# Attention and gated FFN in one kernel: joint q/k loads, causal masks on two engines, x flips in FFN banks, and a new plan of the order

## The chip, the cores and the metric

The kernel runs on one core of one Trainium2 chip. The time is the device time of one execution in microseconds (us), as the median of several executions. One execution does 64 heads of causal attention with decay, and then a gated FFN over 4,608 tokens.

The engines are called by the profile's names: PE is TensorE (matmul), PEld its weight load, DVE VectorE, ACT ScalarE, POOL GpSimd, SP SyncE.

## The reference, cut to what matters

```python
B, H, S, D = 8, 8, 576, 64                          # q, k, v: [B, H, S, D]; f: [B, H, S]
scores = (q @ k.T) / sqrt(D)
cum    = cumsum(log(clip(f, 1e-4, 1)), -1)
scores = where(causal, -1e9, scores + cum[..., :, None] - cum[..., None, :])
attn   = softmax(scores)                            # the maximum is taken off first
x      = (attn @ v) -> [B*S, H*D] = [4608, 512]
g      = x @ w_gate                                 # [4608, 1536]
out    = (g * sigmoid(g) * (x @ w_val)) @ w_out     # [4608, 512]
```

## The kernel before: the parts that the change touches

The program is not written in its order of execution. Each piece of work is an `op` with a modelled duration, the ops it must follow, the buffers it takes and a priority (`key`). A small event simulation (`Plan`) then decides on the host in which order each engine's instructions are emitted. So a changed duration in the model, or a changed constant, moves instructions on every engine. Cuts are marked.

```python
# two heads ("a pair") of q or k per load, from GpSimd's queue
def ld_qk(e, p, nm, b):
    nc.gpsimd.dma_start(out=nat[b.pool][b.i],
        in_=srcs[nm][2 * p : 2 * p + 2].rearrange("h (p t) d -> p h (t d)", t=QT))

# "turn": q or k is transposed on TensorE; "straighten": PSUM -> QK on ScalarE or VectorE
bn, bt = Buf("natw" if b == 1 else "nat"), Buf("t", ("f", BORROW), ("s", 22.0))
o1 = op(("POOL", 0.64), ld_qk, p, nm, bn, take=[bn], key=kk, dma=0.74, ...)
o3 = op(("PE", mm(*[QP] * QT)), turn, bn, bt, after=[o1, o_id], take=[bt], use=[bn], ...)
# ... cut

# one bank of scores: matmul -> exp -> causal mask -> weighing of V
a = op(("PE", mm(*cols)), score, h, i, bs, ...)
a = op(("ACT", act(sum(cols))), expo, h, i, bs, ...)
a = op(("POOL", 0.33), mask, h, i, after=[a], use=[hp], key=kk, ...)     # affine_select on GpSimd
ws.append(op(("PE", mm(*[D + 1] * cells)), weigh, h, i, bo, base, opens, ...))
# ... cut: reciprocal and scaling on VectorE

# "flip": the scaled result is transposed on TensorE and put into xT, which the FFN reads
bt = Buf("t", ("f", BORROW))           # one bank "t"; an FFN bank "f" only until BORROW
a = op(("PE", mm(*[P] * nq)), flip, bx, bt, qb, nq, after=scaled + [o_id], take=[bt], use=[bx], ...)

# idle-filling matmuls on the identity, emitted while the plan sees TensorE without work
def dummy(i):
    z = bank[bank_of["f"] + i]
    nc.tensor.matmul(z[:, :HALF], ident, ident.unsqueeze(1).to_broadcast([P, 2, P]), start=True, stop=True)
span = plan.run((2.0, IDLE_TO, dummy, 0.107))
```

Later on each FFN column chunk needs one chunk of `wg` and `wv` (384 KB each, four chunks, loaded from GpSimd's queue). A "gate" is the group of matmuls with `wg` and `wv`, a "projection" that with `wo`.

The softmax here doesn't subtract the row's maximum and nothing guards it: scores larger than these inputs give would overflow.

## Time and profile before

| kernel before | value |
|---|---|
| median of 3 runs | 405.83 us (403.91 to 407.4) |
| span of the profiled execution | 1431.7 us, not one of the timed runs' kind |
| masks on GpSimd | 256: 192 of one block, 64 of two |
| q/k loads of batches 0 to 2 | 24, two heads each |

Read this page with care: TensorE ran at a quarter of its pace in the profiled execution, which the prediction finds from the matmul durations. The rows below are from the groups of the page and from its loads. The columns are line, engine, operation, output and inputs with shapes, count, then busy us and the mean ns of one; in the load rows the last figure is the median us from issue to landing.

```profile
L662 PE MATMUL ps<-xT,wv 128*128 128x512 bf16 (+3 forms) x480 | 388.7, 1020 | 0.0
...
L547 POOL TENSOR_SCALAR_AFFINE_SELECT PT<-PT 128x128 bf16<-128x128 bf16 (+1 forms) x192 | 52.5, 274 | 473.2 <-ACT PT L538 469.5
L547 POOL TENSOR_SCALAR_AFFINE_SELECT PTa<-PTa 128x256 bf16<-128x256 bf16 x64 | 25.9, 405 | 461.5 <-ACT PTa L538 461.4
...
wg<-in_moe_w_gate_dram POOLq DMA_DIRECT2D x4, 384.0 KB, 7.6
wv<-in_moe_w_val_dram POOLq DMA_DIRECT2D x4, 384.0 KB, 9.3
```

What may be used of such a page: durations of engines other than TensorE (a mask is 0.274 or 0.405 us), and counts. What may not: waits. At this pace TensorE is busy 99% of the span, and the others mostly wait for it.

### The profile page before, as it was taken

The numbers are of one execution on the slowest core, as the hardware profiler recorded it, in microseconds if no ns is written. First come the engines' busy times: TensorE is split into PE (matmuls) and PEld (weight loads), VectorE is DVE, ScalarE is ACT, GpSimd is POOL, SyncE is SP. The second block draws the span as 40 slices with busy tenths as digits, with TensorE's granted clock in tenths as the row PEclk, the third lists the DMA queues.
The fourth block names the chain that finished last, engine by engine and source line by source line (L and its number), as shares of the span: only waits on it lengthen the run. The fifth ranks groups of instructions, "written<-read, shape, count | busy, mean of one in ns | idle before, by whom it ended". The sixth has DMA issues, their size and how long they took to land.

```text
span 1431.7 us, 8507 instructions
## 1 busy us (share of the span) xinstructions
PE 1424.2 (99%) x3189; PEld 569.1 (40%) x3189; DVE 233.2 (16%) x447; ACT 237.5 (17%) x444; POOL 135.1 (9%) x370
## 2 busy tenths in 40 slices
PE   9999999999999999999999999999999999999998
PEld 6665553344433333343343343434443222222332
DVE  3132220122101210112002110121101210210210
ACT  3322210122112111111111212212221000100000
POOL 5311120101000100010001101100110000000000
DMA  8510210330034003400233012200000000000000
GB/s 140 93 35 9 44 25 22 59 67 0 8 79 76 0 0 79 98 1 17 50 72 64 16 21 51 56 0 1 8 15 8 0 8 22 0 0 29 0 0 26
DMA packets 103897, 46.57 MB, mean 33 GB/s; under 512 B 87792, under 2 KB 98736, under 8 KB 103536
## 3 DMA queue, kind: packets, MB, share of 16 engines
q1 hardware_dynamic: 89440, 31.08, 9.5%
q0 software_dynamic: 11296, 14.16, 6.4%
q10 hardware_dynamic: 3120, 0.79, 0.3%
q8 instruction: 25, 0.41, 0.1%
q14 instruction: 16, 0.13, 0.0%
HBM read 38.34 MB, written 15.78 MB: 38 GB/s over the span
## 4 chain that ended last, share of the span: by engine, by line
PE 99%; POOL 0%; issue 0%; ACT 0%; ACTq 0%; POOLq 0%
PE ps L662 49%; PE ps L677 25%; PE ps L530 11%; PE ps L561 7%; PE ps L585 2%; PE ps L763 2%; PE ps L418 2%; POOL xT L412 0%; ACT ot L681 0%; POOL ident masks.py:199 0%; POOL ident masks.py:197 0%; ACTq L681 0%; POOLq L802 0%
## 5 line engine op out<-in xcount | busy, mean ns | idle before, releaser
L662 PE MATMUL ps<-xT,wv 128*128 128x512 bf16 (+3 forms) x480 | 388.7, 1020 | 0.0
L662 PE MATMUL ps<-xT,wg 128*128 128x512 bf16 (+3 forms) x480 | 387.7, 1016 | 0.0
L677 PE MATMUL ps<-wo,hh 128*128 128x512 bf16 (+1 forms) x444 | 382.9, 1098 | 0.0
L530 PE MATMUL ps<-QK 68*128 68x320 bf16 (+4 forms) x448 | 210.2, 637 | 0.0
L662 PEld LDWEIGHTS <-wv 128*128 128x128 bf16 x480 | 104.5, 221 | 194.5 <-issue 193.1
L662 PEld LDWEIGHTS <-wg 128*128 128x128 bf16 x480 | 99.8, 212 | 199.1 <-issue 198.3
L677 PEld LDWEIGHTS <-hh 128*128 128x128 bf16 (+1 forms) x444 | 94.1, 216 | 206.4 <-issue 204.9
L666 ACT ACTIVATE th<-ps 128x512 f32<-128x512 f32 (+3 forms) x120 | 66.5, 554 | 527.8 <-PE ps L662 527.8
L561 PEld LDWEIGHTS <-PT 128*128 128x128 bf16 x768 | 106.7, 186 | 77.4 <-issue 65.8
L538 ACT ACTIVATE PT<-ps 128x512 bf16<-128x512 f32 (+2 forms) x192 | 96.7, 508 | 242.5 <-PE ps L530 237.1
L670 DVE SCALAR_TENSOR_TENSOR th<-th,ps 128x512 f32<-128x512 f32 (+3 forms) x120 | 75.6, 630 | 357.6 <-ACT th L666 357.5
L673 DVE TENSOR_TENSOR hh<-th,ps 128x512 bf16<-128x512 f32 (+3 forms) x120 | 76.1, 634 | 273.5 <-PE ps L662 273.4
L561 PE MATMUL ps<-VB,PT 128*128 128x65 bf16 x768 | 120.0, 350 | 0.0
L530 PEld LDWEIGHTS <-QK 68*128 68x128 bf16 x448 | 78.5, 197 | 69.6 <-issue 67.4
L547 POOL TENSOR_SCALAR_AFFINE_SELECT PT<-PT 128x128 bf16<-128x128 bf16 (+1 forms) x192 | 52.5, 274 | 473.2 <-ACT PT L538 469.5
L547 POOL TENSOR_SCALAR_AFFINE_SELECT PTa<-PTa 128x256 bf16<-128x256 bf16 x64 | 25.9, 405 | 461.5 <-ACT PTa L538 461.4
L568 DVE RECIPROCAL rc<-ps 128x5 f32<-128x5 f32 (+2 forms) x64 | 12.4, 194 | 328.5 <-PE ps L561 328.4
L681 ACT ACTIVATE ot<-ps 128x512 f32<-128x512 f32 (+1 forms) x37 | 22.1, 597 | 256.0 <-PE ps L677 256.0
L538 ACT ACTIVATE PTa<-ps 128x384 bf16<-128x384 f32 x64 | 31.1, 490 | 130.3 <-PE ps L530 128.5
L561 PEld LDWEIGHTS <-PTa 128*128 128x128 bf16 x192 | 32.1, 194 | 47.0 <-issue 37.0
L585 PEld LDWEIGHTS <-xn 128*128 128x128 bf16 x160 | 33.9, 235 | 33.8 <-issue 32.1
L585 PE MATMUL ps<-ident,xn 128*128 128x128 bf16 x160 | 43.2, 493 | 0.0
(48 smaller groups left out, 295.3 us busy)
## 6 DMA issues: line engine op xcount, KB each, us to landing
out_dram<-ot SPq DMA_DIRECT2D x35, 256.0 KB
natv<-in_v_dram SPq DMA_DIRECT2D x29, 256.0 KB
qk_d<-in_q_dram POOLq DMA_DIRECT2D x5, 576.0 KB, 5.5
qk_d<-in_k_dram POOLq DMA_DIRECT2D x5, 576.0 KB, 5.8
wg<-in_moe_w_gate_dram POOLq DMA_DIRECT2D x4, 384.0 KB, 7.6
wv<-in_moe_w_val_dram POOLq DMA_DIRECT2D x4, 384.0 KB, 9.3
wo<-in_moe_w_out_dram POOLq DMA_DIRECT2D x4, 384.0 KB, 6.3
QK<-qk_d SPq DMA_TRANSPOSE x80
```

The source lines that it names most:

```text
L418: nc.tensor.transpose(t[:, n : n + QP], src[:, h, P * y : P * y + P], ident[:QP, :QP])
L530: nc.tensor.matmul(s[:, c : c + w], QK[:KR, hqk[p].i, 2 * j + 1, kt * P : (kt + 1) * P], QK[:KR, hqk[p].i, 2 * j, q0 : q0 + w], start=True ...
L538: nc.scalar.activation(place(h, i)[:, OFFS[i] : OFFS[i] + c], ps(bs)[:, :c], AF.Exp, scale=0.125)
L547: nc.gpsimd.affine_select(out=d, in_=d, pattern=pat, compare_op=ALU.is_ge, fill=0.0, base=0, channel_multiplier=-1,)
L561: nc.tensor.matmul(o[:, lo : lo + D + 1], pt[:, c : c + P], VB[hvb[b].i][:, kt, hb, : D + 1], start=first and n == 0, stop=last and n == l ...
L585: nc.tensor.transpose(t[:, n * P : (n + 1) * P], XN[bx.i][:, qb + n].rearrange("p h d -> p (h d)"), ident)
L662: nc.tensor.matmul(ps(bf)[:, :n], w[:, ko, fc * P : (fc + 1) * P], xT[:, ko, t0 : t0 + n], start=(ko == 0), stop=(ko == KD - 1))
L666: nc.scalar.activation(TH[bt.i][:, :n], ps(bf)[:, :n], AF.Tanh, scale=0.5)
L670: nc.vector.scalar_tensor_tensor(out=t, in0=t, scalar=1.0, in1=ps(bf)[:, :n], op0=ALU.add, op1=ALU.mult)
L673: nc.vector.tensor_mul(HH[:, bh.i, lo : lo + n], TH[bt.i][:, :n], ps(bf)[:, :n])
L677: nc.tensor.matmul(ps(bf)[:m, :DM], HH[:, hs[fc].i, lo : lo + m], wo[:, fc, :], start=(fc == 0), stop=(fc == KF - 1))
L763: nc.tensor.matmul(z[:, :HALF], ident, ident.unsqueeze(1).to_broadcast([P, 2, P]), start=True, stop=True)
```

## The change

The intent is to shorten the start, in which TensorE is not yet fed: fewer q/k loads on GpSimd's queue, masks that GpSimd and VectorE share, x flips that need not wait for the one bank `t`, and an order found again with corrected durations. The whole diff has some 280 lines; its core:

```diff
-    def ld_qk(e, p, nm, b):
-        nc.gpsimd.dma_start(out=nat[b.pool][b.i], in_=srcs[nm][2 * p : 2 * p + 2]...)
+    def ld_qk(e, p, n, nm, b):                      # n = 1 or 2 pairs per load
+        lo = 2 * (p % 2)
+        nc.gpsimd.dma_start(out=nat[b.pool][b.i][:, lo : lo + 2 * n], in_=srcs[nm][2 * p : 2 * (p + n)]...)
 # ... cut: from pair JOINT = 2 on, an even pair's load brings the odd pair too
+        if e == "DVE":
+            keep = tri.unsqueeze(1).to_broadcast([P, 2, P]) if i == 0 else tri[:, :m]
+            nc.vector.tensor_tensor(out=d, in0=d, in1=keep, op=ALU.min)
+            return
-                    a = op(("POOL", 0.33), mask, h, i, after=[a], ...)
+                    a = op({"POOL": 0.3 if i else 0.42, "DVE": 0.2 if i else 0.34}, mask, h, i, after=[a, o_tri], ...)
-            bt = Buf("t", ("f", BORROW))
+            bt = Buf("t", ("f", BORROW_T if ahead else BORROW))
 # ... cut: V casts of batches 0 and 1 on any of three engines; model costs of loads, exponentials, engine starts
-    span = plan.run((2.0, IDLE_TO, dummy, 0.107))
+    span = plan.run((4.2, IDLE_TO, dummy, 0.107))
-W_AT = [6.8, -9.5, 10.4, 20.2]
+W_AT = [-10.8, 8.4, 17.6, 31.7]                     # when the weight chunks may be issued
-BORROW = 34.7
+BORROW = 23.3
-V0_KEY = (-18.9, -18.8, -14.4, 16.0, -20)
+V0_KEY = (-19.1, 7.5, 26.8, 22.6, 32.0)
+JOINT = 2
+QKEY1 = 1414.1
+BORROW_T = 89.5
 # ... cut: some ten more constants of the plan
```

(`tri` holds 3e38 where a score is kept and 0 where it is masked, so the minimum with it is the mask.)

## The prediction

> **What bounds the kernel now.** I read the page's head and engine totals first, then the groups of instructions with shapes kept apart, then the timeline of the first 75 us and of the last 10.
>
> ```profile
> span 1431.7 us, 8507 instructions
> PE 1424.2 (99%) x3189; PEld 569.1 (40%) x3189; DVE 233.2 (16%) x447; ACT 237.5 (17%) x444; POOL 135.1 (9%) x370
> ...
> L677 PE MATMUL ps<-wo,hh 128*128 128x512 bf16 x420 | 363.4, 1100 | 0.0
> ...
> 265.82 3.20 PE ps L662 x4
> ...
> 280.66 3.36 PE ps L662 x4
> ```
>
> The profiled execution is not the one that was timed: its span is 1431.7 us, the timed median 405.83. Four 512-column matmuls take 3.20 to 3.36 us, about 0.82 us each, so one column takes 1.6 ns. TensorE ran at roughly a quarter of its pace, although the page prints a granted clock of 1.0. So "PE 99%" says nothing about the timed runs. What can be kept are the durations on VectorE, ScalarE and GpSimd and the landing times of the first loads.
>
> For the timed runs I count TensorE's work instead. The columns streamed are: gate and value projections 442,368, output projection 227,328, scores 102,400, weighing of V 62,400, flips 20,480, turns of q and k 13,824; together 868,800 in 3,116 matmuls (the 73 idle-filling matmuls on the identity left out). At the skill's warm pace (below) that is 362.0 + 7.8 = 369.8 us.
>
> The timed run exceeds its span by about 1.8 us (1433.5 against 1431.7), so 405.8 is a span of 404.0.
>
> ```profile
> 1427.75 0.59 ACT L681 ACTIVATE ot<-ps 64x512 f32<-64x512 f32 x1 [9.19 <-PE ps L677]
> ```
>
> The last copy starts 3.9 us before the end: that is the tail. 404.0 - 369.8 - 3.9 = 30.3 us in which TensorE does not do its counted work at the counted pace. The change can only work on those 30 us. Where are they?
>
> ```profile
> L538 ACT ACTIVATE PT<-ps 128x512 bf16<-128x512 f32 x64 | 38.2, 597 | 99.8 <-PE ps L530 98.8 <-PE ps L561 0.9
> L538 ACT ACTIVATE PTa<-ps 128x384 bf16<-128x384 f32 x64 | 31.1, 490 | 130.3 <-PE ps L530 128.5
> ...
> L538 ACT ACTIVATE PT<-ps 128x320 bf16<-128x320 f32 x64 | 28.0, 437 | 59.9 <-PE ps L530 57.1 <-PE ps L561 1.0 <-POOL PT L547 0.3
> ...
> L301 ACT ACTIVATE QK<-ps 64x576 bf16<-64x576 bf16 x22 | 17.7, 805 | 28.3 <-PE ps L418 14.6 <-DVE QK L303 9.3 <-POOL QK L380 4.3
> ```
>
> One head's exponentials are 0.490 + 0.597 + 0.490 + 0.437 = 2.0 us of ScalarE; its TensorE work (scores, weighing, turns, flips: 199,104 columns over 64 heads) is about 1.35 us. Until the FFN's matmuls run, ScalarE sets the pace. I walked the program order and summed measured durations up to each tanh (ScalarE) and counted matmul time up to its gate (TensorE). At the first gate: ScalarE 26.3 us (setup 4.7, eight straightenings 6.4, 30 exponentials 15.2), TensorE 10.9 us. The difference, ScalarE's surplus, is largest at the second gate, 15.95 us, still 14.9 at the eleventh and 12.9 at the 23rd, and falls to 2 once the first output projection (16 us of TensorE work) comes. From there TensorE is the bound to the end. So lost time = surplus + ScalarE's idle time before its steady run + small stalls: 30.3 = 16 + some 8 + some 6.
>
> ScalarE's idle: its first exponential can't start before q and k of the first pair have landed, been turned and straightened, and the decay rows have come.
>
> ```profile
> 1.39 0.78 POOL L412 DMA_DIRECT2D xT<-in_q_dram  x1 [0.88 <-POOLq L802]
> ...
> 5.86 0.66 POOL L412 DMA_DIRECT2D xT<-in_q_dram  x1
> ...
> 8.48 0.70 POOL L412 DMA_DIRECT2D xT<-in_k_dram  x1
> ...
> xT<-in_q_dram POOLq DMA_DIRECT2D x8, 144.0 KB, 4.5
> ```
>
> In this stretch the eight loads took 5.5 to 6.8 us to land, so they land from 6.9 to 14.4 us. VectorE ends the scans at 9.8 and straightens then; GpSimd's clearing of QK (0.97 us) stands between the first straightening and the next ones; rows go out by some 11.5 us. I put the first exponential of a timed run at 14.8 us (26.9 in the slow profile). ScalarE has worked 8.2 us by then: 6.6 idle, and 1 to 2 more where the second rows come only after the interleaved second chain of decays. That is the 8.
>
> **What the Trainium skill says.** "TensorE: Matmul & The Clock Gate", section "Back-to-back issue gap": warm, a matmul of N columns takes N/2.4 + 2.5 ns. The trace shows four times that; the timed 405.83 us cannot hold the trace's pace and fits the page's. The same page, "Seeing it yourself", reports a clock stuck at a quarter; the trace's 1.6 ns per column fits. "DMA: Bandwidth & Descriptors", "Issuing engines are not separate DMA queues": all queues share the same engines and interleave; the first loads' 5.5 to 6.8 us beside the V loads, against 4.5 as the median of all such q loads, agrees. "VectorE: DVE Perf Modes", "Mode 2×_1P — pack two bf16 into one 32-bit read": a two-tensor bf16 operation can do two elements a cycle; no row of this trace is such an operation, so the VectorE mask is an estimate.
>
> **The change part by part.**
> Useful TensorE work is the same 369.8 us: the order listing shows the same matmuls, with 86 idle-fillers for 73. These fill time in which it would wait, so they cost nothing by themselves.
>
> Joint loads: q/k load issues fall from 24 to 14, about 10 x 0.65 = 6.5 us of GpSimd. Bytes are unchanged. In the first batch pair 0 comes alone, then pairs 2 and 3 in two loads of double size, then pair 1. At the spacing of the old loads (some 0.8 us per 144 KB) all are in at about 14 us, as before; the gain is GpSimd time: the first weights are issued at about 8.3 us (1.4 + six loads at 0.65 + identity and triangle 1.1 + clearing 1.7, rounded) instead of 14.5. They were not the wait: the first wg and wv landed by 22.3 us in the trace, and the first gate of the old plan cannot come before 33.
>
> Masks: 81 of 256 move to VectorE at an estimated 0.34 (256 wide) or 0.2 us: +19.4 us there, 78.5 to 53.3 on GpSimd. GpSimd is not the bound in either case. Its gain is a shorter exponential-to-weighing latency early on; VectorE becomes busier precisely where it was not free.
>
> Order: the new plan reaches the first gate after 16 exponentials instead of 30, with 6.7 us of TensorE work done and 21.2 us of ScalarE work. That looks like a large gain and is not: the surplus is only put off. ScalarE's is 14.4 at the first gate and peaks at 15.4 (eleventh) against 15.95: 0.5 us better. VectorE's, which peaked at 12.4, now peaks at 16.2 (sixteenth gate). So ScalarE and VectorE are both full there.
>
> Start: seven straightenings, a V cast and both decay rows are put ahead of the first exponential, which I place at 15.8 us, with 11.3 us of ScalarE work done: 4.5 idle instead of 8. VectorE, waiting for f (3.8 us in the trace) and the loads, idles about 5.5. Bound of the new plan: max(15.4 + 4.5, 16.2 + 5.5) = 21.7; of the old: 15.95 + 8 = 24. That is 2.3 us. The flips in FFN banks take away waits of the single transpose bank in batch 0: about 1 us. Steady state, where over 300 us are TensorE's, gains nothing. Sum: 2.3 + 1 = 3.3, so 405.8 - 3.3 = 402.5 us.
>
> **The rivals.**
> (a) VectorE takes over as the bound: two full engines in a chain (exponential, mask, weighing, reciprocal, scaling, flip, copy) stall each other. VectorE's surplus speaks for it; the plan weighing the mask's cost speaks against. It eats all: 405 to 408.
> (b) The last weight chunk becomes a wait: the new plan issues wg and wv chunk 4 among late masks, at about 31 us; in the trace these two took 7.6 and 9.8 us to land, so about 41 to 42, when the tenth gate pair needs them. Up to 2 us lost, 404 to 405. The earlier first chunks speak against.
> (c) The old plan's stalls (my 6 us rest) are mostly ScalarE waiting on masks, casts and the transpose bank, and the refitted plan removes them: 5 to 8 us more, 395 to 398. For it: GpSimd holds casts, masks and load issues in one queue early (7.6 of its first 10 us busy). Against: part of the rest must be weight loads beside 65-column matmuls, which do not change.
> (d) Nothing visible: TensorE-bound steady state, start set by the same bytes, 405.
>
> **Range and chances.** 402.5 us, 398 to 407 eight times in ten; the three old runs alone spread from 403.9 to 407.4. Faster by over 2% needs under 397.7, that is 8 of the 30 us, only by (c): 0.15. Slower by over 2% (414) would need (a) and (b) together: 0.04. Within 2%: 0.81.
>
> **What would show it.** In the new profile: the first exponential near 16 us with few gaps on ScalarE after it; VectorE nearly full from 18 us to the first output projection; masks on VectorE near 0.34 and 0.2 us; the first gate earlier by some 6 us yet the first output projection only 2 to 4 us earlier; TensorE gapless afterwards. Wrong if TensorE shows gaps in the later batches (then the rest is not where I put it), if the tenth gate waits for a weight load (b), or if VectorE masks take GpSimd's 0.4 us or more (a). A profile at a quarter clock again would show none of the waits, only durations and landings.

## The result, and the profile after

| | before | changed |
|---|---|---|
| first measurement, median of 4 runs | 406.18 us (403.91 to 407.4) | 400.91 us (400.31 to 401.91) |
| ratio (95% interval) | | 0.9879 (0.983 to 0.9929) |
| repeated later (e8 below) | 405.29 us (11 runs) | 400.31 us (6 runs), ratio 0.9886 (0.9857 to 0.9914) |

So the change is worth 1.1 to 1.2%, some 5 us: within 2%, and inside the range. The point of 402.5 us was 1.6 us too slow.

The profile of the changed kernel came at full clock. To have a partner for it, the kernel before was profiled once more without any edit; that is the first run below, and its profile is used from here on. First the changed kernel's page, its head and two rows of the span cut into 40 slices of 10 us:

```profile
span 400.2 us, 8519 instructions
...
PE 387.2 (97%) x3157; PEld 227.5 (57%) x3202; DVE 248.0 (62%) x526; ACT 223.2 (56%) x451; POOL 101.6 (25%) x276
...
PE   5899999999999999999999999999999999999996
...
PEclk9989999999999999999999999999999999999999
```

The same lines of the kernel before, profiled again:

```profile
span 403.9 us, 8464 instructions
...
PE 386.4 (96%) x3146; PEld 227.3 (56%) x3189; DVE 229.8 (57%) x447; ACT 220.3 (55%) x444; POOL 134.2 (33%) x370
...
PE   6679999999999999999999999999999999999996
...
PEclk9997999999999999999999999999999999999999
```

The spans differ by 3.7 us. The two PE rows differ in the first three slices only, 5 8 9 against 6 6 7; from the fourth on (30 us) both are full to the end. The clock rows show one dip each: 7 in the fourth slice of before, 8 in the third of the changed kernel. GpSimd has 33 us less to do and VectorE 18 us more, and neither shows in the time by itself.

The stretches of the start, first for the kernel before. The columns are the stretch, its length, then busy us (and instructions) of PE, PEld, DVE, ACT and POOL, the granted clock, the DMA share and GB/s; the sum is over the first 75 us, of which the rows 0 to 10, 50 to 60 and 60 to 75 us are left out.

```profile
core 0: us, PE busy (x) PEld busy (x) DVE busy (x) ACT busy (x) POOL busy (x), PEclk, DMA share, GB/s
...
10.00:20.00 10.00, 6.10 (x80) 5.09 (x77) 8.47 (x13) 8.09 (x14) 9.33 (x21) 1.00 1.17 176
20.00:30.00 10.00, 7.77 (x77) 5.42 (x76) 3.41 (x12) 7.04 (x19) 6.56 (x22) 0.98 1.36 181
30.00:40.00 10.00, 9.68 (x131) 8.46 (x132) 4.14 (x11) 6.77 (x16) 7.43 (x28) 0.68 1.27 207
40.00:50.00 10.00, 9.05 (x114) 7.85 (x112) 8.73 (x21) 7.31 (x18) 7.34 (x17) 1.00 0.93 199
...
sum 75.00, PE 63.87 PEld 51.38 DVE 50.96 ACT 52.70 POOL 52.65; mean PE 9.12 PEld 7.34 DVE 7.28 ACT 7.53 POOL 7.52
```

And for the changed kernel:

```profile
10.00:20.00 10.00, 8.76 (x87) 7.11 (x86) 7.34 (x12) 7.49 (x12) 4.29 (x20) 1.00 1.30 202
20.00:30.00 10.00, 9.81 (x93) 7.40 (x92) 6.32 (x24) 7.89 (x21) 4.10 (x10) 0.83 1.33 182
30.00:40.00 10.00, 10.00 (x158) 9.05 (x156) 8.36 (x23) 9.08 (x21) 5.76 (x14) 1.00 1.22 205
40.00:50.00 10.00, 10.00 (x128) 8.33 (x125) 9.22 (x22) 8.91 (x22) 3.99 (x13) 1.00 0.57 90
...
sum 75.00, PE 68.83 PEld 53.71 DVE 56.49 ACT 56.24 POOL 38.78; mean PE 9.83 PEld 7.67 DVE 8.07 ACT 8.03 POOL 5.54
```

TensorE is busy 68.83 us of the first 75 instead of 63.87. (Busy is not useful: it holds idle-fillers, and at half clock the same work counts twice as long.) Between 30 and 50 us the changed kernel's TensorE has no gap at all, while ScalarE and VectorE are 84 to 92% busy; before, TensorE lacked 1.3 us there, and VectorE was 41% busy in 30 to 40.

To see where time is lost I took, at each weight load of the two traces, the time so far less the useful TensorE work done so far (useful: the prediction's count, 2.4 columns per ns and 2.5 ns a matmul):

| time lost up to ... | before | changed |
|---|---|---|
| 3 us of useful work | 15.2 | 16.8 |
| 6 us | 20.4 | 21.5 |
| the first gate, at 36.3 us before and 28.5 changed | 25.8 | 22.2 |
| 20 us before, 25 changed | 27.2 | 22.9 |
| first output projection, at 75.4 and 68.0 us | 27.8 | 23.4 |
| the end | 29.8 | 26.0 |

The changed kernel starts worse by 1 to 2 us. Then the kernel before loses another 5.4 us between 6 and 12 us of useful work, at 26.5 to 37.8 us, where the changed kernel loses 0.7. After the first projection both lose only 2.0 to 2.6 us in 330. Nearly all of the loss is in the start, as predicted.

What happens there in the kernel before? The chain of waits, by line, names a transfer that the changed kernel's doesn't have:

```profile
PE ps L662 46%; PE ps L677 24%; PE ps L530 10%; PE ps L561 7%; DMA natv<-in_v_dram 2%; PE ps L585 2%; DMA xT<-in_f_dram 1%; PE ps L418 1%; DVE QK L303 1%; DVE xT L340 0%; ACT QK L301 0%; DVE xT L327 0%; ACT PT L538 0%; POOL QK L380 0%; DVE xT L337 0%
```

The timeline of SyncE's queue and then of GpSimd, kernel before (start us, us, engine, line, operation, output and inputs, count, and in brackets the idle time before it and what ended it):

```profile
8.13 11.83 SPq L356 DMA_DIRECT2D QK<-xT  x8
20.01 0.71 SPq L445 DMA_DIRECT2D natv<-in_v_dram  x1
```

```profile
28.75 0.61 POOL L303 CAST VB<-natv 64x512 bf16<-64x512 f32 x1 [3.44 <-DMA natv<-in_v_dram]
```

The fifth V load, of only 64 rows, was issued at 20.0 us, behind eight decay-row transfers. GpSimd stood 3.4 us for it with a dozen masks queued behind its cast. TensorE (kernel before) felt it:

```profile
28.91 0.38 PE L530 MATMUL ps<-QK 68*128 68x192 bf16 x2 [0.20 <-ACT PT L538]
30.32 0.46 PE L561 MATMUL ps<-VB,PT 128*128 128x65 bf16 x5 [1.03 <-POOL PT L547]
...
36.36 0.60 PE L662 MATMUL ps<-xT,wg 128*128 128x256 bf16 x4
```

From 30.3 us on TensorE had no gap, but its clock was halved. Stretches cut at the changes of the clock, kernel before:

```profile
26.12:29.53 3.41, 2.83 (x19) 1.00 1.45 146
29.53:32.94 3.41, 2.62 (x31) 0.50 1.28 191
32.94:36.35 3.41, 3.41 (x40) 0.50 1.27 196
```

Here the columns after the length are PE's busy us and count, the clock, the DMA share and GB/s. Six us of gapless work at half clock (30.3 to 36.35) cost 3.0 us, and TensorE's idle time between 26.4 and 30.3 us is 1.3 us; of the 5.4 us lost, some 1 us is not broken down. The Trainium skill, "TensorE: Matmul & The Clock Gate", Part 1, "What's actually happening", describes such a gate: half or full rate, decided in a free-running window of 3413 ns. These traces agree: each halved stretch lasts 3.4 or 6.8 us, one or two such windows, and its date shifts from run to run (20.0 to 21.4 us in the four traces of the changed start that have one: the changed kernel's, e4, e5 and e8).

The changed kernel has one such stretch in its first profile, at 20.2 to 23.6 us, and a gate at 28.6:

```profile
8.82 4.04 PE L792 MATMUL ps<-ident 128*128 128x256 bf16 x18
12.66 1.01 PE L432 MATMUL ps<-ident,xT 96*128 96x96 bf16 x12
13.50 2.35 PE L792 MATMUL ps<-ident 128*128 128x256 bf16 x20
...
19.50 0.50 PE L555 MATMUL ps<-QK 68*128 68x256 bf16 x4 [0.90 <-DVE QK L310]
...
28.61 0.60 PE L691 MATMUL ps<-xT,wg 128*128 128x256 bf16 x4
```

Its first exponential stands on ScalarE at 19.12 us, not at the predicted 15.8:

```profile
16.97 2.29 ACT L308 ACTIVATE QK<-ps 64x576 bf16<-64x576 bf16 x3 [1.62 <-DVE QK L310]
19.12 0.47 ACT L563 ACTIVATE PTa<-ps 128x384 bf16<-128x384 f32 x1
```

In the order of TensorE, the turns of pairs 2 and 3 stand behind 18 fillers (L792), and the next turns behind 20 more. Their q had landed at 9.7 us (issued at 3.3, landed 6.3 later) and was turned at 12.66. ScalarE then waited 1.6 us for a straightening on VectorE. By its first exponential ScalarE had worked 11.2 us, as predicted (11.3), but stood idle for 7.9 us where 4.5 were predicted: 4.1 of them behind VectorE's first work on `f`, 2.0 for straightenings on VectorE, 1.3 before its first instruction. The kernel before has 8.0 us of such idle time by its first exponential, so the new plan saved none of it.

**The start runs at half pace, and the clock row does not show it.** In the trace of the changed kernel and in those of all the experiments the first fillers (256 columns) start 213 ns apart; from some moment on it is 109 ns. That moment is 9.1 us for the kernel before (e0), 13.4 for the changed kernel, and 6.4 to 14.6 over all of them. The profile's clock records only begin there; so the row prints 9 for the half-pace time, and a run's mean clock does not hold it either. In the changed kernel's trace the 18 fillers before the turns therefore took 3.8 us instead of 2.0. Were they what held the turns up? e10 below has the same 18 fillers, but full pace from 8.8 us:

```profile
8.61 2.22 PE L810 MATMUL ps<-ident 128*128 128x256 bf16 x18
11.69 0.67 PE L443 MATMUL ps<-ident,xT 96*128 96x96 bf16 x12 [0.87 <-ACT QK L308]
```

There the turns waited for ScalarE behind the fillers, and the first exponential came at 18.53 us, only 0.6 us earlier. So the pace of the first 18 fillers accounts for at most some 0.6 of the 3.3 us. The next 20 stand for 2.2 to 2.3 us in the chain of waits of both traces; whether the turns behind them could have run sooner was not tested.

One number of VectorE's new work, from the groups of the changed kernel:

```profile
L574 DVE TENSOR_TENSOR PT<-PT,tri 128x128 bf16<-128x128 bf16 (+1 forms) x58 | 13.7, 236 | 16.8 <-ACT PT L563 16.0
```

**The clock differs from run to run.** One halved window of 3.41 us lowers a run's mean clock by 0.5 x 3.41 / 400 = 0.0043. The clocks recorded with the runs fall into such steps, so I count halved windows per run. This count is an estimate, but the traces fit it: before's at 0.992 holds two such windows, that of e7 below at 0.983 four. It leaves out the half-pace start, which differs from run to run as well.

| halved windows, estimated | before: 33 runs | changed: 10 runs |
|---|---|---|
| 0 (clock 0.998 to 1.000) | none | 8 runs, median 400.34 us |
| 1 (0.994 to 0.996) | 5 runs, 403.60 | 2 runs, 401.92 |
| 2 (0.990 to 0.992) | 15 runs, 404.50 | none |
| 3 (0.986 to 0.987) | 4 runs, 405.46 | none |
| 4 (0.983) | 9 runs, 405.61 | none |

For the kernel before a window costs (405.61 - 403.60) / 3 = 0.67 us, so without any it would take about 402.9 us: an estimate, since no such run exists. By this estimate the 5 us split into some 2.6 us of better order (402.9 against 400.34) and some 2 us of clock: before has 2.5 halved windows a run, changed 0.2.

### The profile page after: what moved, and what is told of

Same layout as the page of the kernel before. It is cut to its first block, busy times and chain, and to the rows that moved or that the text cites. A ratio compares the mean times of both kernels' runs of the same rounds, so it can differ in the third digit from the quotient of the medians.

```text
span 400.2 us, 8519 instructions
## 1 busy us (share of the span) xinstructions
PE 387.2 (97%) x3157; PEld 227.5 (57%) x3202; DVE 248.0 (62%) x526; ACT 223.2 (56%) x451; POOL 101.6 (25%) x276
## 4 chain that ended last, share of the span: by engine, by line
PE 93%; ACT 2%; DMA 2%; DVE 1%; issue 1%; POOL 0%; ACTq 0%; DVEq 0%; POOLq 0%
PE ps L691 46%; PE ps L706 23%; PE ps L555 11%; PE ps L590 7%; PE ps L792 3%; PE ps L614 2%; DMA xT<-in_k_dram 2%; PE ps L432 1%; DVE QK L310 1%; ACT QK L308 1%; ACT PTa L563 0%; ACT ot L710 0%; POOL xT L426 0%; DVE th L699 0%; ACT th L695 0%
## 5 line engine op out<-in xcount | busy, mean ns | idle before, releaser
L691 PE MATMUL ps<-xT,wv 128*128 128x512 bf16 (+3 forms) x468 | 111.4, 357 | 0.6
L691 PE MATMUL ps<-xT,wg 128*128 128x512 bf16 (+3 forms) x464 | 110.8, 357 | 0.9
L706 PE MATMUL ps<-wo,hh 128*128 128x512 bf16 (+1 forms) x427 | 103.3, 379 | 0.9
L555 PE MATMUL ps<-QK 68*128 68x320 bf16 (+4 forms) x448 | 74.6, 262 | 1.2 <-DVE QK L310 0.9
L691 PEld LDWEIGHTS <-wg 128*128 128x128 bf16 x480 | 45.1, 97 | 36.4 <-issue 0.2
L706 PEld LDWEIGHTS <-hh 128*128 128x128 bf16 (+1 forms) x444 | 41.6, 98 | 41.1 <-issue 1.3
L691 PEld LDWEIGHTS <-wv 128*128 128x128 bf16 x480 | 45.0, 97 | 34.2 <-DMA wv<-in_moe_w_val_dram 0.2
L590 PEld LDWEIGHTS <-PT 128*128 128x128 bf16 x768 | 37.4, 97 | 15.2 <-DVE PT L574 0.4
L590 PE MATMUL ps<-VB,PT 128*128 128x65 bf16 x768 | 44.6, 193 | 0.1
L555 PEld LDWEIGHTS <-QK 68*128 68x128 bf16 x448 | 35.3, 98 | 14.5 <-DVE QK L310 1.1
L574 DVE TENSOR_TENSOR PT<-PT,tri 128x128 bf16<-128x128 bf16 (+1 forms) x58 | 13.7, 236 | 16.8 <-ACT PT L563 16.0
```

Of the source, the lines that this page charges most:

```text
L555: nc.tensor.matmul(s[:, c : c + w], QK[:KR, hqk[p].i, 2 * j + 1, kt * P : (kt + 1) * P], QK[:KR, hqk[p].i, 2 * j, q0 : q0 + w], start=True ...
L590: nc.tensor.matmul(o[:, lo : lo + D + 1], pt[:, c : c + P], VB[hvb[b].i][:, kt, hb, : D + 1], start=first and n == 0, stop=last and n == l ...
L691: nc.tensor.matmul(ps(bf)[:, :n], w[:, ko, fc * P : (fc + 1) * P], xT[:, ko, t0 : t0 + n], start=(ko == 0), stop=(ko == KD - 1))
L706: nc.tensor.matmul(ps(bf)[:m, :DM], HH[:, hs[fc].i, lo : lo + m], wo[:, fc, :], start=(fc == 0), stop=(fc == KF - 1))
```

## The experiments

Three calls, each with eleven runs of the kernel before on the same chip. All results were correct. "At full clock" below means the runs with a mean clock of 0.998 or more, median. The calls ran on three chips, on which the kernel before took 405.35, 404.75 and 405.29 us, so half a microsecond between runs of different calls says nothing. The changed kernel's 400.34 us is from the first measurement and the third call.

### e0: the kernel before, unchanged

No edit. The question was what a profile at full clock shows.

> The kernel before, unchanged, to get a profile of it at full clock. Theory S (the prediction's: the lost TensorE time lies before the steady state and is set by ScalarE's work and its idle start): first exponential near 15 us, first gate near 33 us with 10.5 us of TensorE work done, so 22 to 24 us lost by then and more up to the eleventh gate; TensorE has next to no gaps after 60 us. Rival P (small stalls all along the batches): the gaps lie after 60 us, several us of them, and the start is the same as in the changed kernel. Time 406, within 1 per cent.

Measured: 405.99 us, span 403.9 us, clock 0.992. Its lines are shown above. The lost time at the end is 29.8 us, where the prediction's arithmetic had 30.3; and the useful work's pace holds: eight 512-column gate matmuls are 1.73 us in the chain of waits, and 8 x (512 / 2.4 + 2.5) ns is 1.73. So the floor of 369.8 us stands. The late V load and the halved clock were new.

### e1 and e2: the plan without the features, the features without the plan

e1 keeps the new constants and model but takes the features out; e2 keeps the features and goes back to the old model costs and constants. Both let the plan order the work anew.

```diff
 # e1, against the changed kernel
-a = op({"POOL": 0.3 if i else 0.42, "DVE": 0.2 if i else 0.34}, mask, ...)
+a = op({"POOL": 0.3 if i else 0.42}, mask, ...)
-JOINT = 2
+JOINT = 99
-BORROW_T = 89.5
+BORROW_T = 23.3
```

```diff
 # e2, against the changed kernel (cut: the model's other costs and all constants as before)
-W_AT = [-10.8, 8.4, 17.6, 31.7]
+W_AT = [6.8, -9.5, 10.4, 20.2]
-BORROW = 23.3
+BORROW = 34.7
```

> The new planner constants and the new order knobs, but single loads of q and k, every mask on GpSimd, and flips borrowing FFN banks no longer than the turns do. If the gain of 1.2 per cent comes from the other plan (order of loads, first gate after 16 exponentials), this shows 0.985 to 0.992 against before. If it comes from the three features, this is 0.998 or above, as the constants were fitted to a kernel that has the features.

> The three features (joint loads, masks on either engine, flips in FFN banks) with the old planner constants and order knobs. Features theory: 0.985 to 0.992 against before. Plan theory: 0.997 to 1.005.

Measured: e1 405.08 us, ratio to before 1.0006 (0.998 to 1.0032); e2 407.88 us, 1.007 (1.004 to 1.01). Neither half gains. e1 is instructive: five of its six runs have no halved window, and still take 405.02 us. It wins the clock and loses in the order: its trace has lost 27.2 us at the first projection (changed: 23.4). e2 has lost 29.0 by then. So the gain is an interaction of the features with the plan's constants and costs. What neither run can do is to give each feature its share, since both were ordered anew. That was the reason to freeze the order from here on.

### e3: the changed kernel's order, all masks on GpSimd

The plan still believes that 81 masks are VectorE's, so the order of the other engines stays the same; the masks themselves run on GpSimd.

```diff
-        if e == "DVE":
+        if e == "NONE":
             keep = tri.unsqueeze(1).to_broadcast([P, 2, P]) if i == 0 else tri[:, :m]
```

> The changed kernel with its program order kept on TensorE, ScalarE and SyncE, and the 81 VectorE masks put back on GpSimd at the same place. If VectorE is the full engine of the early phase (the prediction has its surplus at 16.2 against ScalarE's 15.4), taking some 3 us of masks off it before the 16th gate makes this as fast or up to 1 us faster than the changed kernel (0.985 to 0.988). If moving masks is what gave the gain by shortening the way from exponential to weighing, it loses 1 to 3 us (0.990 to 0.996).

Measured: 402.0 us, ratio 0.9928 (0.9901 to 0.9954); 401.69 at full clock, against 400.34 for the changed kernel: 1.35 us slower. Had VectorE been the bound (rival a), taking 81 masks off it would have made it faster. (The runs with one halved window agree: 402.85 and 403.54 against 401.91 and 401.92.) Its trace shows a wait that is hardly there in the changed kernel: the last chunk of `wv`. The wait table of PEld, changed kernel, then e3:

```profile
PEld L691 <- DMA wv<-in_moe_w_val_dram: 0.2, 1, 0.2
```

```profile
PEld L691 <- DMA wv<-in_moe_w_val_dram: 1.9, 1, 1.9
```

The columns are total us, times, longest us. That is rival (b), and it is a race of two dates. The `wv` half of the chunk was issued at 35.2 us in the changed kernel and landed 9.4 us later, in e3 at 34.5 us and landed 10.2 later: at 44.6 and 44.7, the same date (predicted: issued at 31). What differs is who asks: in the changed kernel's profile the first gate came at 28.5 us, behind a halved window, in e3, with no halved window, at 26.8, and so the gate that needs the chunk came earlier too. The earlier start is not the masks' work: profiles of this order without a halved window have the first gate at 26.4 to 27.0 us, with one at 28.3 to 29.5. The fair partner of e3 is therefore e9 further down, with this order, its masks on VectorE and no halved window: there the half landed at 43.3 us and TensorE stood 0.4 us for it. In this pair the landing is 1.3 us later with GpSimd's masks (issue 0.8 later, transfer 0.6 longer). One profile each does not show that the masks did it: the unedited changed kernel landed the same half at 44.6 us in its first profile and at 43.5 in e8's.

### e4 and e5: the last weight chunk early, with and without the masks on VectorE

The last `wg`/`wv` chunk is issued some 5 us earlier, behind a clearing on GpSimd at 28 us. e5 adds e3's edit.

```diff
             nc.gpsimd.memset(VB[what][LAST:, NB - 1], 0.0)
+            if what == 1:
+                for t, src in ((wg, w_gate), (wv, w_val)):
+                    tc.no_sync_barrier()
+                    chunk(t, src, NCH - 1)
 # ... cut: the helper chunk; the chunk's old issue is left out
```

> The changed kernel in its own order, but the last chunk of wg and wv issued at about 28 us instead of 34.4 and 35.2 us. Theory W (in the changed kernel the last weight chunk, landing at 44.6 us, and the VectorE masks bind together): TensorE waits only 0.2 us for that chunk here, so alone it gains 0 to 0.3 us against the changed kernel (0.986 to 0.989 against before). Rival theory (the chunk alone binds): 1.5 us or more, 0.984 or less.

> The same early chunk, with the 81 VectorE masks put back on GpSimd. With the masks on GpSimd alone, the first gate came 1.7 us earlier (26.8 against 28.5 us) and TensorE then waited 1.9 us for the last wv chunk. Theory W: that wait goes and the 1.7 us reach the end, span near 398.4, ratio 0.983 to 0.986 against before. Rival (VectorE does not matter, something later holds both): same as the changed kernel, 0.988 or above.

Measured: e4 400.07 us, ratio 0.9911 (0.9876 to 0.9946), 399.9 at full clock; e5 401.43 us, 0.9921 (0.9893 to 0.9949), 400.81 at full clock. In neither trace does TensorE wait for a weight chunk. At full clock e4 is 0.4 us ahead of the changed kernel, which is no more than the chips differ by; over all runs its ratio misses the expected 0.986 to 0.989. e5 misses theory W's ratio (0.983 to 0.986) and falls to its rival, so taking away the wait did not bring the 1.7 us of the earlier gate to the end. Between e4 and e5, where that wait is gone from both, the masks on VectorE gain 0.9 us at full clock (four and three runs), but lose 0.9 us in the runs with one halved window (402.84 against 401.91, two and three runs), and over all runs the intervals overlap. So e3's loss is not confirmed here: rival (a) is refuted by e3 and by the changed kernel's time, while the masks' own worth stays open. At half pace 3.41 us hold 1.7 us less work, so one halved window alone should cost no more than that; e4's runs with one are 2.9 us slower, and its trace has full pace only from 14.6 us, so the half-pace start is likely part of that.

### e6: each joint load issued as two

```diff
-        nc.gpsimd.dma_start(out=nat[b.pool][b.i][:, lo : lo + 2 * n], in_=srcs[nm][2 * p : 2 * (p + n)]...)
+        for m in range(n):
+            nc.gpsimd.dma_start(out=nat[b.pool][b.i][:, lo + 2 * m : lo + 2 * m + 2], in_=srcs[nm][2 * (p + m) : 2 * (p + m + 1)]...)
```

> The changed kernel in its own order, but each joint load of q or k issued as two single loads, one after the other. Same bytes; seven to ten more issues on GpSimd at 0.65 us each, in the start two of them before the last q and k loads, so the last of these go out some 1.3 us later. If joint loads matter for the start: 0.5 to 1.3 us slower than the changed kernel (0.990 to 0.993). If the start hangs on other things (idle-filling matmuls ahead of the turns, straightening on ScalarE and VectorE): within 0.3 us (0.987 to 0.989).

Measured: 401.74 us, ratio 0.9938 (0.9908 to 0.9967); 401.67 at full clock, 1.3 us slower than the changed kernel. PEld's waits, e6:

```profile
PEld L692 <- DMA wv<-in_moe_w_val_dram: 2.1, 1, 2.1
```

The last `wv` was issued at 33.67 us and landed 10.7 us later. Its partner at the same clock, e9, is this:

```profile
PEld L697 <- DMA wv<-in_moe_w_val_dram: 0.4, 1, 0.4
```

There it was issued at 33.70 us, the same date, and landed 9.6 us later. So the joint loads do matter, and in this trace the loss is a wait for the last weight chunk: it landed 1.1 us later than in e9, and the first gate came 0.6 us earlier (26.5 against 27.1). Whether the split makes it land later one profile doesn't tell; the unedited kernel's two profiles have 9.4 and 8.3 us for the same transfer.

### e7: the kernel before with its late V load early

The 64-row V load is issued fourth on SyncE's queue, at 2.7 us instead of 20.0.

```diff
+        if (b, n) == (0, NB - 1):
+            assert bv.i == 4
+            return
         E[e].dma_start(out=natv[bv.i][:m], in_=...)
+        if b == 0 and e == "SP":
+            tc.no_sync_barrier()
+            nc.sync.dma_start(out=natv[4][:LAST], in_=v[0, :, S - LAST :].rearrange("h p d -> p h d"))
```

> The kernel before, in its own order, but the fifth V load (64 rows) of batch 0 issued as the fourth load on SyncE at about 2.7 us instead of at 20 us behind the rows. In the full-clock profile of the kernel before GpSimd stands 3.4 us for that load with twelve masks behind its cast, TensorE stands 1.0 us for the masks and its clock is halved from 29.5 to 36.4 us. Theory V (this one wait is the larger part of the 3.7 us that the change gained): 2 to 3 us faster than before, ratio 0.993 to 0.996. Rival S (ScalarE's pace of exponentials sets the first gate, the V wait is covered): 0.5 us or less, 0.998 to 1.002.

Measured: 402.87 us against 404.75, ratio 0.9968 (0.9933 to 1.0003): the interval just holds 1. That lies between theory V and rival S. The wait is removed (GpSimd's 3.4 us for V and TensorE's 1.0 us for a mask are both gone from its tables), its worth is not settled. With as many halved windows, e7 is faster by 0.9 us at one (402.69 against 403.60, two and five runs), by 0.5 us at four (one run against nine), and not at all at three (405.53 against 405.46, one and four runs). By these pairs the late load explains about a third of the order's gain; the interval leaves room for more.

### e8 to e11: the changed kernel again, more fillers, fillers with the early chunk, and flips without the FFN banks

e8 is the changed kernel with no edit. e9 adds 15 idle-filling matmuls where TensorE's gaps were: three at about 6 us, one at 8, and eleven behind the turns of pair 1 at 17 to 18 us. e10 is e9 with e4's early chunk. e11 gives the flips the same limit as the turns, as before the change, with the order planned anew.

```diff
 # e9 (cut: four more fillers in `dummy`)
+    extra = [3, 8]
     def turn(e, p, bn, bt):
+        if p == 1 and plan.free["o"]:
+            z = bank[bank_of["o"]]
+            for _ in range(extra.pop(0)):
+                nc.tensor.matmul(z[:, :HALF], ident, ident.unsqueeze(1).to_broadcast([P, 2, P]), start=True, stop=True)
 # e11
-BORROW_T = 89.5
+BORROW_T = 23.3
```

> The changed kernel, unchanged, as the reference of this call. Theory C (runs of one kernel fall in two groups by whether TensorE's clock was halved during the start; each run's mean granted clock tells which): runs with a mean clock of 0.998 or more are near 400.4, runs at 0.995 or less 1 to 3 us longer. Ratio against before 0.986 to 0.990. Rival (the spread is noise unrelated to the clock): no such order among the runs.

> The changed kernel in its own order, with 15 more idle-filling matmuls on the identity where TensorE stood in the start (3 and 1 at about 6 and 8 us, 3 and 8 behind the turns of pair 1 at about 17.4 and 18.6 us), to keep its clock from being halved at about 20 us. Theory C: fewer or no runs at a clock of 0.995 or less, first gate near 26.5 us in the profile; but the last wv chunk lands at 44.6 us all the same and TensorE then waits 1.5 to 2 us for it, so the time is that of the changed kernel's better runs, ratio 0.984 to 0.988. Rival: more matmuls in front of the scores only delay them, 0.989 to 0.991.

> The fill and the last wg and wv chunk issued at about 27 us. Theory C with W: a start at full clock, and no wait for the chunk, so the 2 us of the earlier first gate reach the end: span near 397.5 to 398.2, 0.981 to 0.985 against before, faster than both kernels. Rival (something else holds the end at the same place): as the changed kernel, 0.987 or above.

> The changed kernel with flips borrowing FFN banks only until the modelled 23.3 us, as turns do, instead of 89.5. The planner then orders batch 0 and 1 anew from there. If flips in FFN banks carry gain: 0.5 to 2 us slower than the changed kernel (0.990 to 0.995); if not, within 0.5 us of it. As the constants were fitted with the borrowing, a small loss would not settle it.

| | median us (lowest to highest) | ratio to before (95%) | runs with a halved window |
|---|---|---|---|
| before | 405.29 (403.82 to 407.51) | 1 | 11 of 11 |
| e8 changed | 400.31 (399.95 to 401.92) | 0.9886 (0.9857 to 0.9914) | 1 of 6 |
| e9 fillers | 400.29 (399.87 to 401.22) | 0.9882 (0.9854 to 0.9909) | 0 of 6 |
| e10 fillers and early chunk | 399.9 (399.85 to 399.98) | 0.9871 (0.9842 to 0.9899) | 0 of 6 |
| e11 flips in bank t | 403.0 (402.6 to 403.25) | 0.9946 (0.992 to 0.9973) | 0 of 6 |

e8 repeats the result. e9's last `wv` chunk landed at 43.3 us and TensorE waited 0.4 us for it, not the expected 1.5 to 2. What the fillers fill is seen in two stretches of the same times. PE's busy us, count and clock, changed kernel:

```profile
16.77:20.18 3.41, 1.99 (x25) 1.00 1.29 199
20.18:23.60 3.42, 3.42 (x22) 0.50 1.27 190
```

and e9, here with all engines (PE first):

```profile
16.77:20.18 3.41, 3.18 (x37) 2.33 (x34) 1.64 (x3) 3.20 (x6) 0.53 (x2) 1.00 1.29 200
```

In the changed kernel a window in which TensorE is 58% busy is followed by a halved one; e4's, e5's and e8's profiles show the same (58%, then half). With the fillers the stretch is 93% busy and no halving follows. But a low share alone does not bring it: windows with 47% (e6, from 41.3 us) and 52% (e3, from 41.5 us), and with 63 to 66% in the kernel before, were followed by full clock. Over the runs: of the 34 runs of kernels with this start (changed, e3 to e6), 10 have a halved window, of the 12 with fillers none. By chance alone a split as extreme would come some 3 times in 100, so an effect of the fillers on the clock is likely, not proved; on one chip, it is 1 of 6 against 0 of 12, and e11 has 0 of 6 without these fillers. By the median e9 gains nothing, since most runs of the changed kernel are at full clock anyway.

e10 misses its expected ratio and keeps its expected span of 397.5 to 398.2 us, from which I had worked the ratio out wrongly. By the ratio it falls to the rival (0.987 or above). Its page:

```profile
span 398.1 us, 8594 instructions
...
PEclk9999999999999999999999999999999999999999
```

By its median it is the fastest kernel, and the steadiest: six runs within 0.13 us. Against the changed kernel of this call it is 0.4 us ahead by the medians, 0.1%, with overlapping intervals of the ratios to before: no more than a small gain, though each of its six runs is faster than all but one of the changed kernel's ten.

e11 is 2.7 us slower than the changed kernel, without any halved window. Its first gate comes as early as the best (26.5 us, 20.2 us lost), but by the first projection it has lost 25.2 us, where the changed kernel has lost 23.4. In that stretch (26.5 to 72.3 us) TensorE is idle for 2.9 us in e11, its two longest waits, 0.8 us each, being for VectorE; in the changed kernel (28.5 to 68.0 us) it is idle for 0.1. So with the flips in FFN banks TensorE stays fed between gate and projection; the size isn't theirs alone, since e11 was planned anew.

## Why the prediction was right or wrong

- **The floor and where the loss lies: right.** 369.8 us of work, 30.3 us lost against 29.8 in the trace, nearly all ahead of the steady state, where both kernels lose 2.0 to 2.6 us. From a profile at a quarter clock this came out by counting columns.
- **Within 2%, 402.5 us: right in class; the sum is close for mixed reasons.** The order is worth an estimated 2.6 us without halved windows (3.3 between the best groups of each kernel, which don't have the same number of them), against 3.3 predicted. That these two are near is luck in part: 2.3 of the 3.3 were to come from an earlier start of ScalarE and a lower surplus, but the changed kernel starts 1 to 2 us worse, and the gain lies later, at 26.5 to 37.8 us before. The rest of the 5 us is, by the estimate above, the granted clock, for which the sum had no term: it took a timed run to be at full clock throughout.
- **"16 + some 8 + some 6": the 8 was right, the cause of the rest wrong.** The first exponential of before is at 15.5 us (predicted 14.8), with 8.0 us of ScalarE's idle time before it. But "until the FFN's matmuls run, ScalarE sets the pace" fails: ScalarE was busy only 7.0 and 6.8 us of the 10 in 20 to 30 and 30 to 40 us. What was lost there is 5.4 us at 26.5 to 37.8 us, of which 3.0 at half clock and 1.3 idle, most of it for a mask behind a late V load. "The first gate cannot come before 33" holds, it came at 36.3.
- **The start of the new plan: wrong in the step "I place at 15.8 us".** It is 19.1 us, and the term that was mis-sized is ScalarE's idle time, 7.9 us instead of 4.5, mostly waits for VectorE. The loads were not what was late: q of the joint load had landed 3 us before its turn. The fillers ("they cost nothing by themselves") ran at half pace until 13.4 us and were 0.9 us late for a bank that ScalarE had freed at 11.8; with full pace from 8.8 us (e10) the first exponential still came at 18.5. No run took the 38 fillers away, so the cost of the later 20 is open.
- **The bound "max(ScalarE, VectorE)": wrong.** The sum let VectorE's surplus of 16.2 us decide and rival (a) feared it. Masks taken off VectorE gained nothing: 1.35 us slower in e3, no clear difference between e4 and e5; VectorE was 63% busy at 20 to 30 us and 84 to 92% from 30 to 50, with TensorE gapless. Its 58 masks of one block took 0.236 us on the mean (estimated 0.2), the 23 of two blocks 0.293 (0.34), so the term was sized right and used wrongly: a large surplus on one engine is no bound while TensorE does not wait for it.
- **Joint loads gain "GpSimd time" alone: wrong.** The first weights "were not the wait", that holds. But split again the loads cost 1.3 us (e6), and its trace waits 2.1 us for the last weight chunk.
- **Rival (b): real, and mostly avoided.** 0.2 us in the changed kernel, 1.9 and 2.1 us in e3 and e6; "up to 2 us" was the right size. In e4's, e5's and e10's traces it is gone.
- **Flips in FFN banks, "about 1 us": too small.** 2.7 us with the order planned anew (e11).
- **Rival (c), 395 to 398: no.** The stalls did shrink (7.4 us earlier first projection, more than the 2 to 4 predicted; 3.0 us of it is only less work done before it), but 26 us are still lost.

Open: each feature's own share of the 2.6 us, since they interact with the plan; why the features under the old constants are 0.7% slower; what the masks on VectorE are worth by themselves; what sets a halved window off; and how much of the new start the fillers cost.

## What to carry to other kernels

When a profile's clock is wrong, count the useful work and subtract: that gives the loss and often its place, but not its cause; get a profile at the right clock before naming a wait. In a tuned kernel a small transfer late in a queue, or a weight chunk that lands just in time, is found by asking which other part comes earlier now and what it then waits for. And sort runs by their granted clock before comparing tenths of a per cent: here runs with one halved window of 3.4 us were 1.1 to 2.9 us slower than runs without. Look too at the spacing of equal matmuls in the start, which showed a half pace that the clock row did not.

## What the Trainium skill lacked or had wrong

- "TensorE: Matmul & The Clock Gate", "What's actually happening": the half-rate state is listed for idle windows, with no busy share at which it sets in. Here it followed windows in which TensorE was 58% busy (1.99 of 3.41 us, changed kernel), and in the kernel before even 83% (2.83 of 3.41 us), while windows with 47% (e6) and 52% (e3) had none after them; the runs give no such share either. The page calls the ramp at the start under 1% of a typical span and not worth fitting; in these traces half pace lasts from the first matmul at 3.4 us to 6.4 to 14.6 us, and the changes under test are themselves 0.1 to 1.2%.
- The same page, "Seeing it yourself", reports a clock stuck at a quarter for 50 us and more; here a whole execution of 1431.7 us ran at a quarter pace while the profile printed a mean granted clock of 1.000.
- "DMA: Bandwidth & Descriptors", "Anatomy of one DMA — SWDGE (gpsimd) path": its fit of 2.0 us plus bytes over 436e3 gives 2.9 us for 384 KB (an estimate from the page). Beside and behind other transfers the weight chunks took 5.0 to 16.8 us from issue to landing, the last `wv` chunk 7.6 to 13.0; the fit has no term for a loaded case, and the waits of 2 us in e3 and e6 are for such a landing.
